# Linear attention beside a GEGLU feed-forward: the attention denominators spread over four token chunks instead of two

## The chip, the core and the metric

The kernel runs on one core of a Trainium2 chip. The metric is the device time of one execution in microseconds (us). Before the change it is 517.17 us, the median of three runs from 516.37 to 517.38. Traces are of one execution; its span, from the first instruction to the last, is 515.4 us.

## What is computed

```python
x  = A_x                                  # 2048 tokens x 576, bf16
xn = layernorm(x)
q, k, v = split(xn @ wqkv)                # 32 heads of 18
phi = lambda t: where(t > 0, t + 1, exp(t)) + 1e-6
kv  = einsum("bhsd,bhse->bhde", phi(k), v)
z   = sum over tokens of phi(k)
den = phi(q) . z + 1e-6                   # one number per token and head
att = (phi(q) @ kv / den) @ wo
ffn = (gelu(xn @ w_gate) * (xn @ w_up)) @ w_down     # 576 -> 4608 -> 576
out = x + att + ffn
```

The division by den is applied to phi(q) ahead of the product: pn = phi(q) / den. It is then transposed to put its features on the partitions, which gives pqT, and multiplied with M = kv @ wo, a matrix that is the same for all tokens.

## The kernel before

**Attention stage (the first 68 us).** All 16 token tiles of 128 tokens go through layer norm, a transpose to xnT, the products for phi(k) and phi(q) (L254 to L266), and the sums from which kv and z are made. phi(q) of all tiles stays in SBUF as pq, z broadcast over the partitions as zb.

**Feed-forward, four chunks of 512 tokens.** Each chunk (sc) has a gate/up stage and a down stage.

The gate/up stage has 18 blocks (k = 0 to 17, `gu_pair`), each of two units of 128 hidden features. A unit is 18 matmuls on half of TensorE's rows each, in two parts p1 and p2 (L314, L321), so that two run side by side. When p2 ends, ScalarE takes the gelu out of PSUM (L579) and VectorE multiplies it with the other product into hT (L580). Two PSUM banks belong to a unit, eight to the ring of banks.

The weights of a block are read again in every chunk. `load_gu` issues four DMAs on SyncE's queue: wg (256 KB, L162) and the last 64 rows of the gate weights into wr (32 KB, L163), then wu (256 KB, L165) and the other half of wr (32 KB, L166). Four sets of buffers make a ring (`NWBUF = 4`), and in block number blk the loads of block blk + 3 are issued. These reuse the buffers of block blk - 1, so SyncE can issue them when TensorE has ended that block, and they must have landed three blocks later. The first matmul of a unit reads wr (kt = 4 comes first in `first`, L304), the load that is issued last.

In chunk 0 SyncE's queue has more to do: wo in block 1 (L539, L540), one slice of w_down of 432 KB in each block from k = 2 until all twelve are on the way (L546), and parts of M that are moved with DMAs after blocks 7 and 9 (L601, L605).

The down stage multiplies hT of the chunk's four token tiles with w_down (L639) and adds pqT times M in the same PSUM banks (L627, L644). VectorE adds x and SyncE stores the tile (L653 to L657). The first two tiles of a chunk open with `pair` (L627), which reads pqT of these tiles.

**The denominators.** Each token tile n has four jobs, taken in this order from the list `den_jobs` (L550):

- `den_mul` (L369): phi(q) times z, on VectorE.
- `den_inv` (L375 to L377): sum over each head, add epsilon, reciprocal, on VectorE.
- `den_scale` (L389, L395, L398): pn, with copies that fill its last columns, on VectorE.
- `den_transpose` (L401): one transposing DMA from pn to pqT, on SyncE's queue.

There are 16 x 4 = 64 jobs. A job is handed out after the product of a unit (L580) in blocks 1 to 16 of a chunk, two in each block, while the list lasts. So two jobs go to each of 16 blocks, 32 to a chunk, eight token tiles to a chunk: all are done in chunks 0 and 1. A tile's transpose follows at the end of the second of its two blocks, k = 2, 4, ... 16.

**What sets the order.** The schedule is written out: instructions of one engine run in the order in which the program issues them, and SyncE's queue is one such order. Within block k it holds the two halves of `load_gu`, the slice of w_down in chunk 0, and then, where the job is a transpose, the transpose. A transpose waits for VectorE to have written pn.

Of the kernel before, what the change touches and what calls it, by code (L numbers as in the profile page):

```python
# [23 lines left out]
NF = F // P  # L24
# [11 lines left out]
GUB = 2  # L36
# [21 lines left out]
def kernel(  # L58
# [93 lines left out]
    def load_gu(i, part):  # L152

        if i >= NSC * NF // GUB:
            return
        f0 = GUB * (i % (NF // GUB))
        c0, c1 = f0 * P, (f0 + GUB) * P
        if part == 0:
            gu_blocks[i] = (wg_bufs.next(), wu_bufs.next(), wr_bufs.next())
        wg, wu, wr = gu_blocks[i]  # L160
        if part == 0:
            nc.sync.dma_start(wg[:], B_w_gate[0:512, c0:c1].rearrange("(kt p) c -> p kt c", p=P))  # L162
            nc.sync.dma_start(wr[0:HP, :], B_w_gate[512:576, c0:c1])  # L163
        else:
            nc.sync.dma_start(wu[:], B_w_up[0:512, c0:c1].rearrange("(kt p) c -> p kt c", p=P))  # L165
            nc.sync.dma_start(wr[HP:P, :], B_w_up[512:576, c0:c1])  # L166
# [371 lines left out]
    def load_wo():  # L538
        nc.sync.dma_start(wo2[:CR, 0:4, :], A_wo[0:4 * CR, :].rearrange("(c p) j -> p c j", p=CR))  # L539
        nc.sync.dma_start(wo2[:D - 4 * CR, 4, :], A_wo[4 * CR:D, :])  # L540
    wd_loaded = [0]

    def load_wd_slice():
        f0 = wd_loaded[0]
        if f0 < NF:
            nc.sync.dma_start(wd_sb[:, f0:f0 + WDS, :], wd_view[:, f0:f0 + WDS, :])  # L546
            wd_loaded[0] += WDS


    den_jobs = [(job, n) for n in range(NS) for job in (den_mul, den_inv, den_scale, den_transpose)]  # L550

    def gu_pair(sc, k):
        cs = slice(sc * SC, (sc + 1) * SC)
        blk = sc * (NF // GUB) + k
        wg, wu, wr = gu_blocks.pop(blk)
        units = []
        for i in range(GUB):
            b = [banks.next(), banks.next()]
            fcol = slice(i * P, (i + 1) * P)

            def lhs(a, rows, kt, fcol=fcol):
                if kt == 4:
                    return wr[rows, fcol]
                return (wg, wu)[a][rows, kt, fcol]

            u = _Unit([ps_all[:, b[0], :], ps_all[:, b[1], :]], lhs, lambda a, rows, kt: xnT[rows, kt, cs],
                      nc.sync if blk == 0 else nc.gpsimd)
            if blk > 0:
                load_gu(blk + NWBUF - 1, i)
            u.p1()  # L570
            units.append((b, u))
        if sc == 0 and k == 1:
            load_wo()
        elif sc == 0 and k >= 2:
            load_wd_slice()
        for i, (b, u) in enumerate(units):
            u.p2()
            gl = fwork.tile([P, SC], F32, name="gl")
            nc.scalar.activation(out=gl[:], in_=ps_all[:, b[0], :], func=ACT.Gelu_apprx_tanh)  # L579
            nc.vector.tensor_tensor(out=hT[:, GUB * k + i, :], in0=ps_all[:, b[1], :], in1=gl[:], op=ALU.mult)  # L580
            if den_jobs and 0 < k < NF // GUB - 1:
                job, n = den_jobs.pop(0)
                job(n)

# [74 lines left out]
    for sc in range(NSC):  # L659
        for k in range(NF // GUB):  # L660
            gu_pair(sc, k)
            if sc == 0 and k in m_last_steps:
                m_last_steps[k]()
        while wd_loaded[0] < NF:
            load_wd_slice()

        tiles = [_DownTile(sc * TPC + j) for j in range(TPC)]
        tiles[0].pair()
        tiles[1].pair()
        spare = tiles[2].banks + tiles[3].banks  # L670
        hooks = {8 + 6 * c: (lambda c=c: m_product(c, lambda hf: spare[(2 * c + hf) % 4])) for c in range(4)} if sc == 0 else {}
        for j, t in enumerate(tiles):
            if j == 2 and sc == NSC - 1:
                tiles[2].pair()
                tiles[3].pair()
            closed = t.opened
            for hf in range(2):
                t.down(hf, hooks if j == hf == 0 else {})
                if closed:
                    t.add(hf)  # L680
        for t in tiles[2:]:
            if sc < NSC - 1:
                t.opened = True
                t.pair()
                for hf in range(2):
                    t.add(hf)
# [30 lines left out]
```

## Time and profile before

| | us |
|---|---|
| median of three runs | 517.17 |
| span of the trace | 515.4 |
| attention stage, up to the first gate/up matmul | 68.45 |
| gate/up stages, chunks 0 to 3 | 73.47, 69.93, 69.93, 69.93 |
| down stages, chunks 0 to 3 | 40.65, 39.90, 39.91, 43.23 |

The stages are cut at the first matmul of the next one. A block of the gate/up stage takes 69.93 / 18 = 3.885 us. The DMA rows of the page (40 slices of 12.9 us; tenths of the 16 DMA engines' time, then GB/s) show where transfers crowd:

```profile
DMA  6543929999920045666500165555000455540000
GB/s 209 143 65 61 248 58 242 249 259 263 247 58 14 1 139 141 191 162 172 151 13 13 37 173 161 153 148 160 25 24 1 130 163 147 155 123 1 13 11 24
```

Slices 6 to 10 of this row, counted from 0, are chunk 0's gate/up stage. How to read the other views: a group of instructions is named by its line, its engine and what it writes and reads, with its count, busy time and mean time. "SPq" is SyncE's queue, where a DMA's row is the time of its issue; the data lands later. A wait is named by who waited and what came last, with the sum in us, how many times, and the longest. The chain of waits is followed back from the last instruction to what released each step.

### The profile page before, as it was taken

The page shows a single profiled execution, that of the slowest core. Times are in us where ns is not written, and L with a number is a line of the kernel's source. Part 1 is how long each engine was busy: PE and PEld are TensorE (multiplying, and loading weights), DVE is VectorE, ACT ScalarE, POOL GpSimd, SP SyncE. Part 2 cuts the span into 40 slices and gives each one's busy share as a digit, 9 for nine tenths or more (in the row PEclk, how much of TensorE's full clock was granted, in tenths as well). Part 3 has the DMA queues.
Part 4 walks back from the last instruction along what each step waited for, and adds up shares of the span by engine and source line. Part 5 has one row for each costly group of instructions (what it writes and reads, how often), then busy time and mean ns, then how long its engine had stood idle before and what let it go on. Part 6 is the DMA issues. An engine that isn't in the chain of part 4 may idle for free.

```text
span 515.4 us, 10597 instructions
## 1 busy us (share of the span) xinstructions
PE 508.2 (99%) x4487; PEld 307.6 (60%) x4487; DVE 207.9 (40%) x446; ACT 136.8 (27%) x267; POOL 6.6 (1%) x23
## 2 busy tenths in 40 slices
PE   8999999998999999999999999999999999999997
PEld 7888854443487744444577644444777544445775
DVE  7886447666610046776510143343100333333101
ACT  5887523232220013323200032332000133222000
POOL 3000000000000000000000000000000000000000
PEclk9999999999999999999999999999999999999999
DMA  6543929999920045666500165555000455540000
GB/s 209 143 65 61 248 58 242 249 259 263 247 58 14 1 139 141 191 162 172 151 13 13 37 173 161 153 148 160 25 24 1 130 163 147 155 123 1 13 11 24
DMA packets 118921, 61.18 MB, mean 119 GB/s; under 512 B 25554, under 2 KB 118042, under 8 KB 118874
## 3 DMA queue, kind: packets, MB, share of 16 engines
q1 hardware_dynamic: 118730, 60.36, 45.1%
q8 instruction: 35, 0.57, 0.5%
q10 hardware_dynamic: 144, 0.15, 0.1%
q14 instruction: 12, 0.10, 0.1%
HBM read 52.79 MB, written 2.36 MB: 107 GB/s over the span
## 4 chain that ended last, share of the span: by engine, by line
PE 94%; DMA 4%; SPq 1%; DVE 1%; issue 0%; ACT 0%
PE ps_all L309 50%; PE ps_all L639 27%; PE ps_all L254 8%; PE ps_all L285 4%; PE ps_all L644 3%; DMA wr<-in_B_w_up_dram 3%; DMA x_sb<-in_A_x_dram 1%; PE ps_all L627 0%; SPq L165 0%; SPq L163 0%; SPq L162 0%; PE ps_all L356 0%; PE ps_all L590 0%; DVE stats L203 0%; PE ps_all L239 0%
## 5 line engine op out<-in xcount | busy, mean ns | idle before, releaser
L309 PE MATMUL ps_all<-xnT,wg 64*128 64x512 bf16 x1152 | 272.4, 376 | 0.0
L309 PE MATMUL ps_all<-xnT,wu 64*128 64x512 bf16 x1152 | 270.2, 376 | 0.0
L579 ACT ACTIVATE gl<-ps_all 128x512 f32<-128x512 f32 x144 | 86.0, 597 | 314.2 <-PE ps_all L309 289.9
L580 DVE TENSOR_TENSOR hT<-ps_all,gl 128x512 bf16<-128x512 f32 x144 | 99.4, 690 | 136.8 <-ACT gl L579 136.5
L309 PEld LDWEIGHTS <-wg 64*128 64x128 bf16 x1152 | 108.1, 94 | 67.7
L309 PEld LDWEIGHTS <-wu 64*128 64x128 bf16 x1152 | 107.8, 94 | 67.9
L639 PE MATMUL ps_all<-wd_sb,hT 128*128 128x288 bf16 x1152 | 147.1, 286 | 0.0
L639 PEld LDWEIGHTS <-hT 128*128 128x128 bf16 x1152 | 112.3, 98 | 29.3 <-issue 1.2
L653 DVE TENSOR_TENSOR res<-ps_all,x_sb 128x288 bf16<-128x288 f32 x32 | 13.8, 455 | 146.4 <-PE ps_all L644 88.2
L309 PE MATMUL ps_all<-xnT,wr 64*128 64x512 bf16 x288 | 57.7, 376 | 2.0 <-DMA wr<-in_B_w_up_dram 2.0
L254 PE MATMUL ps_all<-wqkv_sb,xnT 128*128 128x288 bf16 x320 | 42.1, 286 | 0.1
L254 PEld LDWEIGHTS <-xnT 128*128 128x128 bf16 x320 | 30.5, 98 | 7.5 <-ACT xnT L243 0.4
L261 ACT ACTIVATE phi_e<-ps_all,neg 128x288 f32<-128x288 f32 x64 | 30.8, 496 | 8.9 <-PE ps_all L254 6.3
L309 PEld LDWEIGHTS <-wr 64*128 64x128 bf16 x288 | 15.1, 94 | 20.1 <-DMA wr<-in_B_w_up_dram 3.5
L285 PE MATMUL ps_all<-hT,xn 128*128 128x288 bf16 (+4 forms) x176 | 22.6, 275 | 0.0
L644 PE MATMUL ps_all<-m_sb,pqT 128*128 128x288 bf16 x128 | 20.9, 286 | 0.0
L285 PEld LDWEIGHTS <-xn 128*128 128x128 bf16 (+1 forms) x176 | 17.6, 101 | 3.9
L266 DVE SCALAR_TENSOR_TENSOR pq<-phi_e,ps_all 128x288 bf16<-128x288 f32 x32 | 14.2, 448 | 7.6 <-ACT phi_e L261 7.2
L266 DVE SCALAR_TENSOR_TENSOR hT<-phi_e,ps_all 128x288 bf16<-128x288 f32 x32 | 14.1, 450 | 2.3 <-ACT phi_e L261 2.3
L644 PEld LDWEIGHTS <-pqT 128*128 128x128 bf16 x128 | 12.5, 98 | 3.2
L203 DVE BATCH_NORM_STATS2 stats<-x_sb 128x6 f32<-128x288 bf16 x32 | 13.6, 440 | 1.9 <-DMA x_sb<-in_A_x_dram 1.9
L389 DVE SCALAR_TENSOR_TENSOR pn<-pq,den_d 128x504 bf16<-128x504 bf16 (+1 forms) x32 | 13.1, 450 | 0.0
(56 smaller groups left out, 105.6 us busy)
## 6 DMA issues: line engine op xcount, KB each, us to landing
wg<-in_B_w_gate_dram SPq DMA_DIRECT2D x72, 256.0 KB, 3.0
wu<-in_B_w_up_dram SPq DMA_DIRECT2D x72, 256.0 KB, 3.7
wd_sb<-in_B_w_down_dram SPq DMA_DIRECT2D x12, 432.0 KB, 5.9
wr<-in_B_w_gate_dram SPq DMA_DIRECT2D x72, 32.0 KB, 3.0
wr<-in_B_w_up_dram SPq DMA_DIRECT2D x72, 32.0 KB, 3.1
out_dram<-res SPq DMA_DIRECT2D x15, 144.0 KB, 1.8
wqkv_sb<-in_A_wqkv_dram SPq DMA_DIRECT2D x3, 576.0 KB
x_sb<-in_A_x_dram SPq DMA_DIRECT2D x5, 288.0 KB, 3.2
```

The lines of the kernel that those rows point to most:

```text
L203: nc.vector.bn_stats(out=ln_raw[n][:, h, :], in_=x_sb[:, n, h * HALF:(h + 1) * HALF])
L254: nc.tensor.matmul(ps_all[:, KQ_BANK[which] + hf, :HALF], lhsT=xnT[:, kt, n * P:(n + 1) * P], rhs=wqkv_sb[:, kt, c:c + HALF], start=(kt == ...
L261: nc.scalar.activation(out=e[:], in_=ps_all[:, KQ_BANK[which] + hf, :HALF], func=ACT.Exp, bias=neg1[:], scale=1.0,)
L266: nc.vector.scalar_tensor_tensor(out=(pq, pk)[which][:, n, hf * HALF:(hf + 1) * HALF], in0=e_tiles[n, which, hf][:], scalar=1.0, in1=ps_al ...
L285: nc.tensor.matmul(ps_all[:m, b, col:col + w], lhsT=xn[:, n, j0:j0 + m], rhs=pk[:, n, d0:d0 + w], start=(n == 0 and col == 0), stop=(n == ...
L309: return nc.tensor.matmul(self.outs[i], lhsT=self.lhs(i, rows, kt), rhs=self.rhs(i, rows, kt), start=start, stop=stop, skip_group_check=True,)
L389: nc.vector.scalar_tensor_tensor(out=pn_c[:, c0:c1, :nh * DH].rearrange("p c (h e) -> p c h e", e=DH), in0=chunked(heads(pq[:, n, h0 * DH: ...
L579: nc.scalar.activation(out=gl[:], in_=ps_all[:, b[0], :], func=ACT.Gelu_apprx_tanh)
L580: nc.vector.tensor_tensor(out=hT[:, GUB * k + i, :], in0=ps_all[:, b[1], :], in1=gl[:], op=ALU.mult)
L639: nc.tensor.matmul(self.acc(hf), lhsT=hT[:, f, j * P:(j + 1) * P], rhs=wd_sb[:, f, HALVES[hf]], start=(f == 0 and not paired), stop=False, ...
L644: nc.tensor.matmul(self.acc(hf), lhsT=pqT[:, c, self.ts], rhs=m_sb[:, c, HALVES[hf]], start=False, stop=(paired and c == 3), skip_group_ch ...
L653: nc.vector.tensor_tensor(out=self.res[:, hs], in0=self.acc(hf), in1=x_sb[:, self.n, hs], op=ALU.add)
```

## The change

Where a job was handed out after each unit of a block, it is handed out after the second unit alone:

```diff
@@ gu_pair
             nc.scalar.activation(out=gl[:], in_=ps_all[:, b[0], :], func=ACT.Gelu_apprx_tanh)
             nc.vector.tensor_tensor(out=hT[:, GUB * k + i, :], in0=ps_all[:, b[1], :], in1=gl[:], op=ALU.mult)
-            if den_jobs and 0 < k < NF // GUB - 1:
+            if den_jobs and i == 1 and 0 < k < NF // GUB - 1:
                 job, n = den_jobs.pop(0)
                 job(n)
```

With one job per block, 16 jobs or four token tiles fall to each chunk, and all four chunks get their share. They are the chunk's own four tiles, each ready before the down stage that reads it. In a chunk, tile j takes blocks 4j + 1 to 4j + 4: den_mul, den_inv, den_scale and den_transpose, one block each. The transposes are issued in blocks 4, 8, 12 and 16. The jobs, their instructions and their number are unchanged. It is meant to even out the load of VectorE and of the DMA queue, heaviest in the first two chunks.

## The prediction

> **What bounds the kernel now.** I read the page first, then the windows by stage, then the waits and the chain inside the one stage that stands out, then the DMA queue's own timeline there.
>
> TensorE carries the span. The first part of the page:
>
> ```profile
> PE 508.2 (99%) x4487; PEld 307.6 (60%) x4487; DVE 207.9 (40%) x446; ACT 136.8 (27%) x267; POOL 6.6 (1%) x23
> ```
>
> VectorE has 60% of its time free, so moving its work helps only where that work holds something else up. The windows of the four gate/up stages (chunks 0 to 3; columns: length, then busy time of PE, PEld, DVE, ACT, POOL, clock, DMA share, GB/s):
>
> ```profile
> 68.45:141.92 73.47, 71.49 (x656) 31.64 (x656) 47.30 (x102) 21.69 (x38) 0.00 (x0) 1.00 1.00 231
> 182.57:252.50 69.93, 69.93 (x653) 31.54 (x648) 47.32 (x103) 20.90 (x35) 0.00 (x0) 1.00 0.63 168
> 292.40:362.33 69.93, 69.93 (x654) 31.54 (x648) 25.18 (x39) 20.91 (x35) 0.00 (x0) 1.00 0.55 157
> 402.24:472.17 69.93, 69.93 (x652) 31.54 (x648) 25.18 (x39) 20.91 (x35) 0.00 (x0) 1.00 0.46 132
> ```
>
> This table decides most. Chunk 1 runs two denominator jobs per block and takes 69.93 us, exactly what chunks 2 and 3 take with none: the jobs cost TensorE nothing by themselves. Only chunk 0 is longer, by 3.54 us, and its DMA share is 1.00. Of the 3.54, about 0.46 is the last part of M (L590, which pushes the next gate/up matmul from about 87.82 to 88.28). So 3.08 us is lost time. What it waits for, in the waits of 66 to 146 us:
>
> ```profile
> PEld L309 <- DMA wr<-in_B_w_up_dram: 3.5, 3, 1.2
> PE ps_all L309 <- DMA wr<-in_B_w_up_dram: 2.0, 3, 0.7
> ```
>
> Three stops, each for the last of a block's four weight loads. The records show 2.0 us idle; each stop also costs the overlap of the row tiles: at the first, matmuls stop at 115.49 and resume at 116.57, 1.08 us. Three of about 1.03 make the 3.08. Why the load was late, from the chain:
>
> ```profile
> 109.24 0.51 SPq L162
> 109.80 0.55 SPq L163
> 110.41 0.58 SPq L165
> 111.04 5.49 DMA wr<-in_B_w_up_dram
> 116.57 2.34 PE ps_all L309 x19
> ```
>
> These are the loads issued in block k=9 for block 12. Their buffers came free at the end of block 8, at 68.45 + 0.46 + 9 x 3.885 = 103.88 us, but SyncE came to them only at 109.24, 5.36 us late. From the start of block 9 to that of block 12 are 3 x 3.885 = 11.66 us. Late start 5.36, plus 1.80 to the issue of the fourth load, plus 5.49 to its landing is 12.65: 0.99 too much, the stop just seen. SyncE's timeline shows where it fell behind:
>
> ```profile
> 78.95 0.37 SPq L546 DMA_DIRECT2D wd_sb<-in_B_w_down_dram  x1
> 81.90 1.25 SPq L401 DMA_TRANSPOSE pqT<-pn  x1
> 83.25 0.51 SPq L162 DMA_DIRECT2D wg<-in_B_w_gate_dram  x1
> ```
>
> and VectorE's, the last instruction that writes pn:
>
> ```profile
> 81.69 0.18 DVE L398 COPY pn<-pn 128x64 bf16<-128x64 bf16 x1
> ```
>
> The transpose sits at the head of SyncE's queue until pn is written at 81.87; the weight load behind it could have gone at 80.11 and goes at 83.25. SyncE's waits in this stage name it again:
>
> ```profile
> SPq L401 <- DVE hT L580: 7.4, 5, 3.1
> SPq L401 <- DVE den_t L369: 2.9, 2, 1.6
> SPq L401 <- DVE den_d L377: 1.1, 1, 1.1
> ```
>
> **What the Trainium skill says.** "Perfetto Trace Analysis", DMA Instruction — HWDGE: the semaphore wait is the sequencer's own and lies outside the profiled window, and it is free for the next instruction only after its descriptors are generated. The trace agrees: 2.58 us between the issues at 79.32 and 81.90, and nothing from behind gets out. The same page, What "DMA-bound" means, tells a limit on the DMA engines from one on the issuing sequencer. Here both are close: SyncE's issues are back to back and the share is 1.00. "Advanced Engine Details and Errata", X-Bar Transpose (TRN2), calls transposing DMAs as fast as regular ones. This trace does not agree: SyncE's queue in chunk 1 took 62.1% of the stage for 11.64 MB, in chunk 2 54.6% for 10.85 MB. The difference, 8 transposes, is 5.2 us for 0.79 MB, 151 GB/s, against 284 GB/s for the rest (10.85 MB in 38.2 us). I take 0.66 us of all 16 engines per transpose.
>
> **The change part by part.**
> VectorE: no instruction is added or removed. A token tile costs 0.75 + (0.74 + 0.18 + 0.35) + (0.82 + 0.17 + 0.18) = 3.19 us by the groups; four tiles leave each of chunks 0 and 1 (-12.8 us) and four come to each of chunks 2 and 3 (25.18 becomes some 37 of 69.93 us). One block needs 1.38 us for its two products and at most 1.27 for its job, of 3.885. Cost and gain: zero, hidden under TensorE, as chunk 1 shows with twice as much. ScalarE's waits for VectorE (17.0 us in chunk 1) shrink, also for nothing.
>
> SyncE in chunk 0, where the gain is. Five issues of a block (wg, wr, wu, wr, wd) take 86.74 to 89.67 = 2.93 us, a transpose with its gaps 89.67 to 91.15 = 1.48. Before: 2 x 2.93 + 1.48 = 7.34 of every two blocks' 7.77, a slack of 0.43 that one wait for VectorE eats. After: 4 x 2.93 + 1.48 = 13.20 of four blocks' 15.54, a slack of 2.34. The wait itself goes as well: now pn is written in the same block as the transpose is queued; after the change den_scale runs after the products of block 3 (about 86.6 us, from a block end near 84.0 plus 1.5 plus 1.2), and SyncE reaches the transpose behind block 4's loads, at about 87.0. So the remaining waits are the loads' own, for TensorE. Rolling the queue forward with these durations, m_last's DMAs included (1.5 us at k=7, 1.2 at k=9): block 7's loads start when their buffer is free, 96.1; block 8's at 96.1 + 2.93 + 1.5 = 100.5; block 9's at 100.5 + 2.93 + 1.48 = 104.9; block 10's at 104.9 + 2.93 + 1.2 = 109.1, where the buffer is free at 107.8. That 1.3 us is the latest start, instead of 7.3 (k=11: 118.94 against 111.65). With the landing as slow as before, 1.3 + 1.8 + 5.5 = 8.6 of 11.66: 3.1 us to spare, and no stop remains. Gain: 3.08 us.
>
> The DMA engines in chunk 0. Four transposes less are 4 x 0.66 = 2.6 us. But the loads now come sooner: 0.590 MB of gate/up and 0.442 MB of wd per 3.885 us are 266 GB/s, 277 with the transposes' time added. What the engines can do I bound from both sides. From 83.25 to 96.96 SyncE issued 4.13 MB while landing went from about 4.0 to 5.8 us: 4.13 x 11.9/13.7 in 13.7 us is 262 GB/s, 275 with its transpose. From 76.36 to 126.45 eleven blocks and six transposes got through, 230 GB/s, or 250 without the transposes' time, but SyncE was held up then. I take 275: balanced, no growing backlog. At 250 the backlog grows by 10% of 46.6 us, 4.5 us, and 1.5 us of stops come back.
>
> Chunks 1 to 3. Chunk 1 stays at 69.93; it had no stop to lose. Chunks 2 and 3 get four transposes each, 2.6 us of engine time at shares of 0.55 and 0.46, and 1.48 us of SyncE every four blocks, where now it mostly waits for TensorE. Chunk 1 carries eight without a stop. Zero.
>
> New due times. Tiles of a chunk are now transposed in the same chunk, at k=4, 8, 12 and 16. Tiles 0 and 1 open the down stage, ready some nine blocks (35 us) early; tile 3, issued in block 16, is first read at least 20 us after the stage begins (two tiles of 10 us). That the wait is by tile, not for the whole of pqT, shows in chunk 0: tile 7's transpose, issued at 139.47 with 2.9 us to landing, was in flight when L627 began at 141.3. Zero. Nothing else moves.
>
> Sum: 517.17 - 3.08 = 514.1 us.
>
> **The rivals.**
> The DMA engines are the bound, not the queue's order. Speaks for it: a share of 1.00 and landings of 5 to 6 us. Against: the starts late by 5 to 7 us, with waits for VectorE behind them. Then 1.0 to 2.0 us of stops stay: 515.1 to 516.1, about 515.6.
> Nothing comes of it: other waits (m_last's copies, transposes that still hold the queue) keep all three stops: 517.2. Against: 2.34 us of slack per four blocks.
> Slower: the transposes moved to chunks 2 and 3 delay weight loads there or a down stage waits for pqT. At one stop of 1.03 us in each and chunk 0 one stop better: 517.17 + 2.06 - 1.03 = 518.2. Against: chunk 1.
>
> **How the numbers follow.** All stops gone, 514.1: 0.66. Part remains, 515.6: 0.20. Nothing, 517.2: 0.07. Slower, 518.2: 0.07. Median times scatter by some 0.5 us, so the first case covers 513.5 to 514.7. The range 513.5 to 516.2 holds the first two; the last two, 0.14, stay out with a little below. The bound of 0.2% is 1.03 us, at 516.14: faster 0.84 (part of the second rounds off), same 0.09, slower 0.07.
>
> **What would show it.** Right: the first gate/up stage at about 70.4 us, no PE wait for wr in it, wg loads starting at most some 2 us after TensorE frees their buffer, transposes there that wait for nothing in VectorE, and the other stages at 69.93. Wrong: late starts gone but landings of 7 to 9 us and stops still there (engines are the bound); stops in chunks 2 or 3, or L627 or L644 waiting for a pqT transpose, would prove the slower case.

## The result

| | us, median | range |
|---|---|---|
| before, runs beside the changed kernel | 516.9 | 516.37 to 517.51 (6) |
| changed | 514.45 | 514.07 to 515.02 (6) |

The ratio is 0.9953, 95% interval 0.994 to 0.9965: faster by 0.5%. The prediction was 514.1 in a range from 513.5 to 516.2.

### Profile after

Part 1 of the page, engines by busy time:

```profile
PE 507.3 (99%) x4487; PEld 307.7 (60%) x4487; DVE 210.8 (41%) x446; ACT 136.7 (27%) x267; POOL 6.7 (1%) x23
```

The four gate/up stages in the windows view (length, then busy time of PE, PEld, DVE, ACT, POOL, clock, DMA share, GB/s):

```profile
68.24:138.61 70.37, 70.37 (x652) 31.70 (x654) 36.62 (x70) 21.47 (x37) 0.00 (x0) 1.00 0.94 240
179.64:249.57 69.93, 69.93 (x653) 31.59 (x648) 37.03 (x71) 20.89 (x35) 0.00 (x0) 1.00 0.65 165
289.48:359.41 69.93, 69.93 (x652) 31.59 (x648) 36.96 (x71) 20.90 (x35) 0.00 (x0) 1.00 0.63 164
399.31:469.24 69.93, 69.93 (x652) 31.59 (x648) 36.95 (x71) 20.90 (x35) 0.00 (x0) 1.00 0.52 142
```

VectorE's work is even now, 37 us in each stage, and chunks 1 to 3 take what they took. Chunk 0 has lost its stops: TensorE is busy in all of its 70.37 us. (This window ends at the first L627. The 73.47 us given for the kernel before end one step later, at the first L639; cut there, the stage is now 138.99 - 68.24 = 70.75 us.) No row of the waits between 66 and 146 us has TensorE waiting for a DMA, and the chain runs through the stage on matmuls alone, broken only by the last part of M at 87.8:

```profile
68.24 19.53 PE ps_all L309 x180
88.14 50.61 PE ps_all L309 x468
```

SyncE's timeline around the first transpose, and VectorE's last write to pn ahead of it:

```profile
87.02 0.59 SPq L546 DMA_DIRECT2D wd_sb<-in_B_w_down_dram  x1
87.70 1.26 SPq L401 DMA_TRANSPOSE pqT<-pn  x1
89.06 0.52 SPq L162 DMA_DIRECT2D wg<-in_B_w_gate_dram  x1
```

```profile
86.22 0.18 DVE L398 COPY pn<-pn 128x64 bf16<-128x64 bf16 x1
```

pn is written at 86.40 and SyncE comes to the transpose at 87.61: it waits for nothing, where it had stood 2.58 us before. The gaps ahead of the four transposes of this stage are 0.09, 0.09, 0.10 and 0.40 us; only the last holds a wait for pn, 0.3 us. The waits view of SyncE can mislead here. Besides those 0.3 us it lists

```profile
SPq L401 <- DVE hT L580: 3.0, 3, 1.2
```

for the three transposes with gaps of 0.09 to 0.10 us. So such a row is not time in which the queue stood; the gaps in the timeline are what I go by.

How late SyncE runs can be read off its timeline. The loads issued in block k have their buffers free at the start of that block, which is the stage's start + 3.885 k, + 0.46 from block 5 on. I take the start of the wg load (L162) minus that, for blocks ahead of the first stop of the kernel before (block 12):

| start of the wg load after its buffer is free, us | k=3 | 5 | 7 | 9 | 11 |
|---|---|---|---|---|---|
| before | 3.1 | 2.8 | 3.3 | 5.4 | 7.3 |
| changed | 0.1 | 0.9 | 0.2 | 1.7 | 1.2 |

A load may start about 11.66 - 1.80 - (4.4 to 5.5) = 4.4 to 5.5 us late before TensorE stops; these are the predicted terms, with the landings of the kernel before.

### The profile page after: what moved, and what is told of

Same layout as the page of the kernel before. It is cut to its first block, busy times and chain, and to the rows that moved or that the text cites. A ratio compares the mean times of both kernels' runs of the same rounds, so it can differ in the third digit from the quotient of the medians.

```text
span 512.4 us, 10601 instructions
## 1 busy us (share of the span) xinstructions
PE 507.3 (99%) x4487; PEld 307.7 (60%) x4487; DVE 210.8 (41%) x446; ACT 136.7 (27%) x267; POOL 6.7 (1%) x23
## 4 chain that ended last, share of the span: by engine, by line
PE 98%; DMA 1%; DVE 0%; ACT 0%; issue 0%
PE ps_all L309 55%; PE ps_all L639 28%; PE ps_all L254 8%; PE ps_all L285 4%; PE ps_all L644 3%; DMA x_sb<-in_A_x_dram 1%; PE ps_all L627 0%; PE ps_all L356 0%; PE ps_all L590 0%; DVE stats L203 0%; PE ps_all L239 0%; ACT xnT L243 0%; DVE res L653 0%; DVE xn L224 0%; PE ps_all L346 0%
## 5 line engine op out<-in xcount | busy, mean ns | idle before, releaser
L639 PE MATMUL ps_all<-wd_sb,hT 128*128 128x288 bf16 x1152 | 147.1, 286 | 0.0
L639 PEld LDWEIGHTS <-hT 128*128 128x128 bf16 x1152 | 112.3, 98 | 29.3 <-issue 1.2
L309 PE MATMUL ps_all<-xnT,wr 64*128 64x512 bf16 x288 | 54.7, 377 | 0.0
```

The source lines that it names most:

```text
L309: return nc.tensor.matmul(self.outs[i], lhsT=self.lhs(i, rows, kt), rhs=self.rhs(i, rows, kt), start=start, stop=stop, skip_group_check=True,)
L639: nc.tensor.matmul(self.acc(hf), lhsT=hT[:, f, j * P:(j + 1) * P], rhs=wd_sb[:, f, HALVES[hf]], start=(f == 0 and not paired), stop=False, ...
```

## The experiments

The theory, called the queue theory: SyncE's queue decides. Loads start late because of what stands ahead of them, and TensorE stops where the lateness passes some 4.4 to 5.5 us. The rival, called the engine theory in what follows: the 16 DMA engines cannot do eight transposes beside the loads of chunk 0, in whatever order they are issued. Each run's own stage in its profiled execution stands in the table at the end.

### The wait taken away, all eight transposes kept

The kernel before, but each transpose is issued at the end of the next block:

```diff
-    den_jobs = [... for job in (den_mul, den_inv, den_scale, den_transpose)]
+    den_jobs = [... for job in (den_mul, den_inv, den_scale, den_later)]   # den_later: tp_due.append(n)
...
+        due = tp_due[:]
+        tp_due.clear()
         for i, (b, u) in enumerate(units):
...
+            if i == 1:
+                for n in due:
+                    den_transpose(n)
```

> The kernel before (two jobs per block, eight transposes in chunk 0), with each transpose issued one block later, so that SyncE finds pn written. It takes away the wait for VectorE and leaves the number of transposes. Queue theory (late starts come from what stands in SyncE's queue): rolled forward, the largest late start falls from 7.3 us to about 3.0, the first gate/up stage is 70.4 us with no stop, 514.5 us. Engine theory (the 16 DMA engines cannot do the transposes beside the loads): the engines have the same to do as before, so two or three stops stay, 516.5 to 517 us.

Measured: 514.54 us, ratio to before 0.9960 (0.9945 to 0.9976). The whole gain in the median, with not one transpose less (one of the six executions took 516.35). Its stage in the windows, and SyncE's queue in the DMA view of the same stage (packets, MB, share of 16 engines):

```profile
68.47:138.87 70.40, 70.40 (x652) 31.60 (x654) 46.92 (x102) 21.48 (x37) 0.00 (x0) 1.00 1.05 241
```

```profile
q1 hardware_dynamic: 29961, 16.83, 104.7%
```

A DMA share above that of the kernel before (1.00), VectorE as busy as before (46.92), and no stop. (The share adds up the time that packets took, and can pass 1, as here.) The rival falls as an explanation: neither the engines' load nor VectorE's own time makes the stops. The largest late start up to block 11 is 3.4 us, where 3.0 was expected.

### The wait put back, with four transposes

The changed kernel, with den_scale after the first unit of blocks 4, 8, 12 and 16 and den_transpose after the second:

```diff
-            if den_jobs and i == 1 and 0 < k < NF // GUB - 1:
+            if den_jobs and 0 < k < NF // GUB - 1 and (i == 1 and k % 4 != 3 or i == 0 and k % 4 == 0):
```

> The changed kernel, with den_scale and den_transpose of a tile in the same block again (k = 4, 8, 12, 16): four transposes per chunk, each waiting for VectorE at the head of SyncE's queue. If the wait alone makes the stops: some of the stops return, 515.5 to 517 us. If it takes the wait and eight transposes together (my roll of the queue): late starts of up to 3.5 us after each transpose, made up within four blocks, no stop, 514.5 us. Engine theory: four transposes as in the changed kernel, 514.5 us.

Measured: 514.44 us, ratio 0.9955 (0.9943 to 0.9967), the changed kernel's time. SyncE's timeline at the first transpose:

```profile
86.46 0.59 SPq L546 DMA_DIRECT2D wd_sb<-in_B_w_down_dram  x1
89.25 1.25 SPq L401 DMA_TRANSPOSE pqT<-pn  x1
90.61 0.52 SPq L162 DMA_DIRECT2D wg<-in_B_w_gate_dram  x1
```

The queue stands from 87.05 to 89.25, 2.20 us, and the next loads start 2.7 us late; 3.7 us is the most up to block 11, 4.0 at block 13. The gaps ahead of its four transposes add up to 5.1 us, more than the 4.5 of the eight in the kernel before. It costs nothing. So the wait alone is not the cause either: halving the transposes, or removing the wait, is each enough.

### The m_last DMAs moved to ScalarE

The kernel before; the third thing in the crowded queue, the copies of M after blocks 7 and 9, goes elsewhere:

```diff
-            nc.sync.dma_start(m_sb[CR + i:CR + i + 1, 0:4, :], m_last[HP + 4 * i:HP + 4 * i + 4, :])
+            nc.scalar.dma_start(m_sb[CR + i:CR + i + 1, 0:4, :], m_last[HP + 4 * i:HP + 4 * i + 4, :])
...
-            nc.sync.dma_start(m_sb[rows, 4, :], m_last[0:HP, :])
+            nc.scalar.dma_start(m_sb[rows, 4, :], m_last[0:HP, :])
```

> The kernel before, with the four DMAs that move m_last issued from ScalarE instead of SyncE. All eight transposes, their waits and all bytes stay; SyncE's queue loses 2.7 us of issues after blocks 7 and 9. Queue theory: the wait for VectorE alone keeps starts some 3.3 us late and no later, since a late queue finds pn written; no stop or one short one, 514.5 to 515.2 us. Engine theory: nothing changes, 516.9 us.

Measured: 516.81 us, ratio 0.9999 (0.999 to 1.0009): no gain. Taken alone it speaks for the rival. The timeline of ScalarE, then of SyncE, shows that the edit did more than was meant:

```profile
100.78 4.09 ACTq L601 DMA_DIRECT2D m_sb<-m_last  x2
104.97 1.08 ACT L579 ACTIVATE gl<-ps_all 128x512 f32<-128x512 f32 x2 [4.37 <-PE ps_all L309]
```

```profile
105.15 0.72 SPq L546 DMA_DIRECT2D wd_sb<-in_B_w_down_dram  x1
107.48 1.22 SPq L401 DMA_TRANSPOSE pqT<-pn  x1
```

Issuing two small DMAs held ScalarE for 4.09 us, where SyncE needs 1.38 (99.00 to 100.38 in the changed kernel). Most of it was not issuing: the two issues took 1.20 and 0.60 us, and ScalarE stood 2.29 us between them. After block 9 two more held it for 2.85 us, with 1.73 us between, and there the chain names what the second issue, at 112.04, waited for: one of SyncE's loads, issued at 108.80.

```profile
108.80 3.22 DMA wg<-in_B_w_gate_dram
```

The gelus behind the issues came late, so VectorE wrote pn late, and SyncE stood at block 8's transpose from 105.87 to 107.48, 1.61 us, where in the kernel before it stood 0.18 there. The queue was rid of 1.4 us and stood 1.4 longer; at block 11 its loads start 7.0 us late, as before. The run could not tell the theories apart. The next does.

### The m_last DMAs moved in time

The kernel before; the same four DMAs stay on SyncE, after the slices of w_down are through:

```diff
-    m_last_steps = {4: m_last_product, 7: m_last_tails, 9: m_last_rows}
+    m_last_steps = {4: m_last_product, 14: m_last_tails, 15: m_last_rows}
```

> The kernel before, with the DMAs that move m_last issued after blocks 14 and 15 instead of 7 and 9; they stay on SyncE, so ScalarE is left alone. All eight transposes, their waits for VectorE and all bytes stay in the stage; only 2.7 us of issues leave the crowded part of SyncE's queue. Queue theory: starts stay some 3.3 us late, as the wait for VectorE makes them, plus up to 1 us where an issue is stretched; with 1.8 + 5.5 that is at most 11.6 of 11.66 us: no stop or one short one, 514.5 to 515.5 us. Engine theory: nothing that the engines do changes, the three stops stay, 516.7 us.

Measured: 514.39 us, ratio 0.9960 (0.9948 to 0.9973). All eight transposes and their waits are there, the denominators are untouched, and the gain is that of the change (one of the five executions took 515.52). Its stage, and SyncE at block 4's transpose:

```profile
67.93:138.33 70.40, 70.40 (x652) 31.67 (x654) 46.90 (x102) 21.47 (x37) 0.00 (x0) 1.00 0.95 233
```

```profile
88.63 0.59 SPq L546 DMA_DIRECT2D wd_sb<-in_B_w_down_dram  x1
89.31 1.50 SPq L401 DMA_TRANSPOSE pqT<-pn  x1
90.91 0.53 SPq L162 DMA_DIRECT2D wg<-in_B_w_gate_dram  x1
```

From the first transpose on, loads start 2.2 to 3.5 us late up to block 11 and no more: a queue that is late finds pn written (88.63 + 0.59 is 0.09 ahead of the transpose), so the wait sets the lateness back to about 3 us but does not add it up. What the queue cannot work off are the 2.7 us of issues after blocks 7 and 9 on top. The engines had a small part in it: in the kernel before, SyncE also stood 0.67 and 0.55 us ahead of the first two loads of block 8, and its waits put these down to earlier DMAs that had not landed; here no such wait is left. (After blocks 14 and 15 they make starts 5.3 and 5.7 us late, but what is loaded then is for chunk 1, a whole down stage away.)

### More to issue, few bytes

The changed kernel with 24 loads of 32 KB more in chunk 0:

```diff
             load_wd_slice()
+            if k <= 13:
+                for _ in range(2):
+                    nc.sync.dma_start(small_w.next()[:], B_w_gate[512:576, 0:GUB * P])
```

> The changed kernel, with two more loads of 32 KB on SyncE's queue in each of blocks 2 to 13, of weights that nothing reads, as large as those of wr (0.56 us each with the gap). 24 loads are 13.4 us of issue but only 0.79 MB, 2.8 us of the engines at 284 GB/s. Queue theory: a block now takes 2.93 + 1.12 + 0.37 = 4.42 us of SyncE's time against 3.885; starts fall 6 to 7 us late from block 10 on and stops of some 4 us in all appear: about 518.5 us. Engine theory: about the 2.6 us of engine time that the change took from chunk 0 comes back, so as before the change, 517 us at most.

Measured: 524.15 us, in one execution. The stops are there as the queue theory has them, but 9.7 us dearer than the changed kernel, not 4. The waits of its TensorE, SyncE's queue over the stage, and two windows of 1 us (the clock stands third from the end):

```profile
PE ps_all L309 <- DMA wr<-in_B_w_up_dram: 2.5, 3, 1.1
PE ps_all L309 <- DMA wr<-in_B_w_gate_dram: 2.4, 2, 1.7
```

```profile
q1 hardware_dynamic: 29764, 17.08, 82.6%
```

```profile
116.00:117.00 1.00, 0.00 (x0) 0.00 (x0) 0.83 (x3) 0.25 (x1) 0.00 (x0) 1.00 1.21 280
120.00:121.00 1.00, 1.00 (x8) 0.39 (x6) 0.00 (x0) 0.00 (x0) 0.00 (x0) 0.50 0.78 230
```

and the median landing of a block's fourth load in this stage, the last number:

```profile
wr<-in_B_w_up_dram SPq DMA_DIRECT2D x16, 32.0 KB, 3.3
```

The engines' share is the lowest of all these kernels, 82.6%, and the stops the worst. The longer stage lowers the share, but the time behind it is not more than the changed kernel's either (0.826 x 80.06 and 0.94 x 70.37 are both 66.1 us), and the fourth loads landed sooner, after 3.3 us against 4.1. So late starts made the stops: SyncE's queue alone can make them. Loads start 11.3 us late at block 11. My reckoning of the queue had it at 6 to 7, since it took every issue at its shortest; the extra loads took 0.47 to 1.30 us each. Much of the rest of the miss is the clock: after each of its two longest stops TensorE ran for some 3 us at half its clock, so the stage lost 9.7 us on 4.9 us of idle PE. I estimate the clock's part at 3.4 us, from the clocks granted in the windows of 1 us between 119 and 144 us.

### More bytes, few issues

The changed kernel with six loads of 288 KB more in chunk 0:

```diff
             load_wd_slice()
+            if k % 2 == 0 and k <= 12:
+                nc.sync.dma_start(spare_w.next()[:], wd_view[:, 0:2, :])
```

> The changed kernel, with one more load of 288 KB on SyncE's queue in each of blocks 2, 4, ... 12, of w_down rows that nothing reads. Six issues of 0.65 us, but 1.77 MB, 6.2 us of the 16 engines at 284 GB/s, more than twice what the change took from chunk 0 (2.6 us). Queue theory: SyncE needs 13.2 + 1.3 of every four blocks' 15.54 us, so starts are late by 2 to 3 us at most; stops come only if landings grow past 7 us; 514.5 to 515.5 us. Engine theory: the engines have more to do than before the change, so at least its three stops come back: 517 us or more.

Measured: 515.44 us, ratio 0.9979 (0.9972 to 0.9986), about 1 us over the changed kernel. The engine theory asked for 517 or more. There is one stop in its profiled execution, at block 16:

```profile
PEld L309 <- DMA wr<-in_B_w_up_dram: 0.8, 1, 0.8
```

The load that came late is one of block 13's, which stood behind a stretched issue, a transpose of 1.74 us:

```profile
123.24 1.74 SPq L401 DMA_TRANSPOSE pqT<-pn  x1
125.08 0.52 SPq L162 DMA_DIRECT2D wg<-in_B_w_gate_dram  x1
```

Loads start up to 5.0 us late (block 13), 2 us more than expected. So 1.77 MB, 6.2 us of engine time by the predicted rate, cost about 1 us. The engines do give some of their delay back to the queue: SyncE's waits for DMAs that had not landed add up to 2.6 us between 66 and 146 us, against 0.2 in the changed kernel. But a load more is not paid for in full.

### All together

| kernel | transposes in chunk 0, waiting for pn | m_last DMAs after blocks | latest start up to block 11, us | first gate/up stage, to the first L639, us | median, us |
|---|---|---|---|---|---|
| before | 8, yes | 7, 9 | 7.3 | 73.47 | 516.5 to 516.9 |
| changed | 4, no | 7, 9 | 2.1 | 70.75 | 514.45 |
| transposes a block later | 8, no | 7, 9 | 3.4 | 70.75 | 514.54 |
| wait put back | 4, yes | 7, 9 | 3.7 | 70.76 | 514.44 |
| m_last in time | 8, yes | 14, 15 | 3.5 | 70.76 | 514.39 |
| m_last on ScalarE | 8, yes, longer | ScalarE | 7.0 | 72.90 | 516.81 |
| more bytes | 4, no | 7, 9 | 4.0 | 71.45 | 515.44 |
| more issues | 4, no | 7, 9 | 11.3 | 80.40 | 524.15 (one run) |

(In the first column "yes" says that the transpose is queued in the block in which pn is written. L601 and L605 are the m_last DMAs. L639 has another number where an edit moved the line.) Up to 3.7 us late, 4.0 in block 13 of the wait put back, costs nothing; 4.0 and then 5.0 in block 13, with more bytes, costs one stop; 7 us and more costs several. No kernel falls out of this order, and the DMA share does not give it. Lateness is known for the profiled execution alone: whether stops came back in the single slower executions of the kernels without one (516.35, 515.52) is open.

## Why the prediction was right, and where not

**What bounds the kernel: right.** Chunk 0 alone had stops, and they were in the loads behind late issues. All other stages came out at 69.93.

**VectorE at nothing: right.** 37 us in the stages of chunks 2 and 3 was forecast, 36.96 and 36.95 measured. (The prediction's own sum, 25.18 + 12.8, gives 38.) Eight tiles in chunk 0 without a stop (46.92 and 46.90 in two of the experiments) show that VectorE's time never counted.

**SyncE's queue: right, and closely.** The step-by-step reckoning had the loads of blocks 8, 9 and 10 start at 100.5, 104.9 and 109.1; they started at 100.48, 105.32 and 109.61, in a stage that itself began 0.21 us earlier. The latest start is 2.1 us late, not 1.3: one issue in block 8 took 1.00 us where 0.51 was assumed.

**The waits rows of SyncE: misread.** The three rows for L401 add up to 11.4 us and were taken as the queue standing for VectorE. The timeline has 4.5 us of gaps ahead of the eight transposes, 2.58 at the first, 0.95 at the third and 0.1 to 0.3 at the others. The argument rests on the gap of 2.58, which is real; but from block 8 on the queue fell further behind through issues, and 1.2 us of waits for earlier DMAs, not through VectorE.

**The engines "balanced, no growing backlog": right in effect.** The fourth load's landing in this stage is 4.1 us in the median, before 4.4. The rival of the engines is settled by the run with all eight transposes. But the price of a transpose, 0.66 us of all engines from the difference of two shares, is not borne out. In chunk 1 four transposes left and the share went up, from 0.63 to 0.65; in chunks 2 and 3 four came and it rose by 0.08 and 0.06, 5.6 and 4.2 us in place of 2.6. It was hidden everywhere, so nothing hung on it. Whether a transposing DMA is slower than a plain one, as the prediction read off that difference, stays open.

**New due times at nothing: right.** No wait for a pqT transpose in any down stage.

**The sum: the mechanism right, one term mis-sized.** The step "Of the 3.54, about 0.46 is the last part of M ... So 3.08 us is lost time" is too large. The end of chunk 0's stage was taken at 141.92, the first L639, while the other stages had been cut ahead of their L627. The chain of the kernel before there, then the timeline of the changed kernel:

```profile
141.58 0.34 PE ps_all L627 x3
141.92 1.09 PE ps_all L639 x8
```

```profile
138.58 0.41 PE L627 MATMUL ps_all<-m_sb,pqT 64*128 64x288 bf16 x4
138.92 0.30 PE L639 MATMUL ps_all<-wd_sb,hT 128*128 128x288 bf16 x1
```

A timeline has the start of a matmul 0.07 us earlier here than the chain, in which the first L639 of the changed kernel starts at 138.99 and its stage at 68.24. Cut at L639 in both, the stage went from 141.92 - 68.45 = 73.47 to 70.75 us. It lost 2.72 us, about 0.91 for each stop where 1.03 was taken; the other 0.36 of the 3.08 are the first matmuls of the down stage, which the changed kernel has as well. (The spans differ by 3.0, with 0.21 from the attention stage. The change does not touch that stage, which ends between 67.93 and 69.11 us in the eight traces.) The medians differ by 2.45: the profiled execution of before took 517.33, one of its longer ones. Executions of before range over 515.75 to 518.28 in the later runs, where those of the changed kernel lie within 514.07 to 515.02. That stops differ from one execution to the next would fit this, but only one was traced. That the forecast time came within 0.4 us is in part luck: the gain was put 0.63 us too high, and the median that it was taken from, 517.17, lay 0.27 above the 516.9 of six runs.

**What the prediction left out.** It named the wait and the number of transposes as two reasons and did not ask whether both were needed. Three things had to come together: eight transposes, their wait, and the m_last DMAs in blocks 7 and 9. With four transposes in place of eight, with no wait, or with the m_last DMAs moved in time, the stops went. The change removed two of the three.

## What to carry to other kernels

When a load lands late, look first at when it was issued and at what stood ahead of it in its queue, then at the engines: compare the start of the issue with the moment its buffer was free, and that lateness with what the ring of buffers can bear. Such a ring hides everything up to its allowance and nothing beyond, so moving any one item out of the crowded stretch can bring the whole gain, and a second one brings no more. In a crowded queue, a DMA that waits for a compute engine belongs one step after its data is ready, not in the same step; where the queue has slack, as with four transposes here, its wait cost nothing.

## What was not expected of the hardware

The DMA share of a stage says little on whether it is bound by DMA: 104.7% without a stop, 82.6% with stops of 4.9 us. Two small DMAs issued from ScalarE while SyncE was issuing held ScalarE for 4.09 us, two more for 2.85, against 1.38 and 1.15 on SyncE; 2.29 and 1.73 us of these were a wait between the two issues. And stops of up to 0.7 us in the kernel before left the granted clock at 1.00, while in the one execution of the kernel with more issues two stretches of 2.7 and 2.2 us with one matmul each (115.6 to 118.3 and 136.6 to 138.9 us) were each followed by some 3 us at a clock of 0.50. A stop of 0.75 us between them left the clock there at 1.00.
